# Pooled attention and a top-1 mixture of experts: the blocked token tiles of a slot scaled two slots ahead, their turns, casts and low parts in a chunk each, and flags read a slot earlier

## The chip, the cores and the metric

The kernel runs on one core of a Trainium2 chip. The time is device microseconds of one launch, with all inputs and the output in device memory. Timed runs are compared by their median; one further execution was profiled.

## The reference

Eight batches of eight heads attend over keys and values that were averaged in groups of eight. The result, 4608 tokens of 512, goes through a mixture of 8 experts, of which each token uses one.

```python
scores = scale * np.matmul(q, k_p.transpose(0, 1, 3, 2))      # k_p, v_p: means of 8 rows
attn = np.exp(scores - np.max(scores, axis=-1, keepdims=True))
attn = attn / (np.sum(attn, axis=-1, keepdims=True) + 1e-09)
x = np.matmul(attn, v_p)                                      # as [4608, 512]
...
logits = x @ w_gate + modality_bias[modality_id]
e_idx = np.argmax(logits, axis=1)
...
for e in range(E):
    mask = e_idx == e
    h = np.maximum(x[mask] @ w1[e], 0.0)
    out[mask] = gate_w[mask, None] * (h @ w2[e])
```

All is in 32 bit floats. w1[e] is 512 x 1024 and w2[e] 1024 x 512.

## The kernel before

The kernel has two stages. The first computes attention and the gates and writes each token's row to `xs` in DRAM: 512 values, its gate weight (column D) and eight factors, one a head (from column RX), by which its values are still to be multiplied. The second stage, the experts, is where the change lies.

**Slots and chunks.** Tokens are sorted by expert into slots of 256 (two tiles of 128 rows, `tt` 0 and 1). Slots 0 to 16 always run; slot 17 runs in one of several forms, here the one called `wide`, in which 384 tokens (a third tile, `xe`) are computed at once. A slot has 8 chunks, `f` 0 to 7, each of 128 hidden units. For a chunk, TensorE (PE) computes the hidden units (`hidden`, L193 and L196), and then the second layer of the chunk before (`second`, L1304), so that ScalarE (ACT) and VectorE (DVE) have one second layer's time to make the hidden units ready. Precision comes from splitting: a value is kept as a rounded high part and the low rest. So each chunk has a fixed chain: ACT copies a half of the sum (`ht`, L198), DVE adds the other half (L199), ACT takes the positive part and rounds it (`hh`, L200), DVE computes the low rest (`hlo`, L202).

**What else a slot needs.** Its tokens are gathered from `xs` by POOL (L144) into `xg`, a ring of four tiles, two a slot. From slot 5 on (`FIRST_BLOCKED`) a slot is "blocked": its tokens are turned (transposed) by DVE rather than by PE. `blocks_out` (L1219) multiplies each tile by its factors on DVE (four instructions, L1227, into a tile `xp` of its own), stores it through SP's queue to `scr` in DRAM (L1231), keeps the gate column in `gc` (L1214), and loads it again so that blocks of 32 x 32 lie where they belong (`y`, L1237). `blocks_turn` turns each block on DVE (L1243) and casts it on ACT (L1245, the high part in `xhl`, for slot 17 `xw`); `blocks_low` computes the low part on DVE (L1250).

**What sets the order.** The order on each engine is the order in which the program is written; each engine works its own list through, and waits by semaphores. `run` (L1342) writes one slot, chunk by chunk. In chunk 0 stand, for slot s + 1: `blocks_out`, the evacuation of the slot before (`tail`: `ob`, L1275 on DVE, L1277 on ACT, scattered by POOL, L1281), and `slot_flag`. The flag says whether slot s + 1 has another expert than slot s. ACT and DVE read it into a register (L1258), and at each chunk they branch on it (`changed`, L1309): if it is set, ACT splits the new weights' high part (L138) and DVE their low part (L141). The functions for the low part wait in a list, `lag`, and are taken up about two chunks later. In chunk 4 stand the gathers of slot s + 2 and the turn and cast of tile 0 of slot s + 1, in chunk 5 the low part of tile 0 and then the turn and cast of tile 1, and so on. Weights are loaded by SP's queue two slots ahead (L128, L131), under a condition, into `raw`.

The end of slot 16 and the first hidden layer of slot 17, which reads `xw`, are written by `close` and `wide`.

Of the kernel before, what the change touches and what calls it, by code (L numbers as in the profile page):

```python
# [9 lines left out]
F32 = mybir.dt.float32  # L10
# [5 lines left out]
ALU = mybir.AluOpType  # L16
# [6 lines left out]
P = 128  # L23
SLOT = 256
EARLY_GROUPS = 2
EARLY_SLOTS = 2
EXTRA = (128,)
QUAD = 32
FIRST_BLOCKED = 5
# [4 lines left out]
def kernel(  # L34
# [12 lines left out]
    nc = tc.nc  # L47
    ctx.enter_context(tc.manual_schedule(engines=ENGINES))
    B, H, S, HD = q.shape
    NTOK, D = out.shape  # L50
    E, _, FF = w1.shape
# [7 lines left out]
    ND = D // P  # L59
    XW = D + 16  # L60
    RX = D + 8
    NSTAT = NTOK // SLOT
# [28 lines left out]
    xg = [cp.tile([P, XW], F32, name=f"xg{i}") for i in range(4)]  # L91
# [57 lines left out]
    def gather(s, idx, col, xgs, rows=NTOK):  # L149
        for tt in range(2):  # L150
            gather_tile(xgs[(2 * s + tt) % 4], idx, col + tt, rows)
# [6 lines left out]
    def scale(s, xgs):  # L158
        for tt in range(2):
            scale_tile(xgs[(2 * s + tt) % 4])  # L160
# [3 lines left out]
    def tokens_of(s):  # L164
        return xhl[s % len(xhl)] if s != NSTAT - 1 else xw
# [52 lines left out]
    with ExitStack() as actx:  # L218
# [661 lines left out]
        for g in range(len(GROUPS) - 1):  # L880
            n = s1_of[2 * g + 1] + 2
# [74 lines left out]
        for n in range(N + 1):  # L956
            has, nxt, nxt2 = n < N, n + 1 < N, n + 2 < N
# [82 lines left out]
    mp = ctx.enter_context(tc.tile_pool(name="mp", bufs=1))  # L1040
# [3 lines left out]
    op = [[ps_op.tile([P, 512], F32, name=f"op{i}_{z}") for z in range(2)] for i in range(2)]  # L1044
# [9 lines left out]
    xe = xg[4]  # L1054
# [142 lines left out]
    def do_late(s, f):  # L1197
        for fn in late.get((s, f), ()):
            fn()

    scr = dram.tile([2, 3 * P, D], F32, name="scr")
    gc = mp.tile([P, NCOL], F32, name="gc")
    ys, yts = {}, {}
    NQ = P // QUAD

    def tts_of(s):
        return (0, 1) if s != NSTAT - 1 else (0, 1, 2)

    def blocked(s):
        return FIRST_BLOCKED <= s < NSTAT  # L1210

    def keep_gates(s, eng):
        for tt in range(2):
            eng.tensor_copy(gc[:, 2 * s + tt:2 * s + tt + 1], xg[(2 * s + tt) % 4][:, D:D + 1])  # L1214

    def gate_of(s, tt):
        return gc[:, 2 * s + tt:2 * s + tt + 1] if s > EARLY_SLOTS else xg[(2 * s + tt) % 4][:, D:D + 1]

    def blocks_out(s):  # L1219

        tts = tts_of(s)
        for tt in tts:
            x = xg[(2 * s + tt) % 4] if tt < 2 else xe
            xp = mp.tile([P, NQ, ND, QUAD], F32, tag="xp", bufs=2, name=f"xp_{s}_{tt}")
            f = x[:, RX:RX + H].rearrange("p (k a o q) -> p k a o q", a=2, o=1, q=1)
            for a in range(2):
                nc.vector.tensor_tensor(  # L1227
                    xp[:, 2 * a:2 * a + 2].rearrange("p j k r -> p k j r"),
                    x[:, 0:D].rearrange("p (k a j r) -> p a k j r", k=ND, a=2, j=2)[:, a],
                    f[:, :, a].to_broadcast([P, ND, 2, QUAD]), op=ALU.mult)  # L1230
            nc.sync.dma_start(scr[s % 2, tt * P:(tt + 1) * P, :], xp.rearrange("p j k r -> p (j k r)"))  # L1231
        keep_gates(s, nc.vector)
        n = len(tts) * NQ
        ys[s] = mp.tile([P, n, P], F32, tag="bid", name=f"y_{s}")
        src = scr[s % 2, 0:len(tts) * P, :].rearrange("(u c) (j x) -> j c u x", c=QUAD, j=NQ)
        for j in range(NQ):
            nc.sync.dma_start(ys[s][j * QUAD:(j + 1) * QUAD], src[j])  # L1237

    def blocks_turn(s, tt):
        ab = tokens_of(s)  # L1240
        sl = slice(tt * P, (tt + 1) * P)
        yt = yts[s, tt] = mp.tile([P, ND, P], F32, tag="bsel", name=f"yt_{s}_{tt}")
        nc.vector.transpose(yt.rearrange("p k (u c) -> p u k c", c=QUAD),  # L1243
                            ys[s][:, NQ * tt:NQ * (tt + 1), :].rearrange("p u (k r) -> p u k r", r=QUAD))
        nc.scalar.copy(ab[:, :, 0, sl], yt)  # L1245

    def blocks_low(s, tt):
        ab = tokens_of(s)
        sl = slice(tt * P, (tt + 1) * P)
        nc.vector.tensor_sub(ab[:, :, 1, sl], yts[s, tt], ab[:, :, 0, sl].bitcast(F32))  # L1250

    def slot_regs(s):
        load_regs(s, meta[0:1, 1 + s:2 + s], meta[0:1, 2 + NSLOT + s:3 + NSLOT + s])
# [3 lines left out]
    def slot_flag(s):  # L1257
        flags[s] = nc.values_load(meta[0:1, 2 + NSLOT + s:3 + NSLOT + s],  # L1258
                                  engines=[mybir.EngineType.Activation, mybir.EngineType.DVE], min_val=0, max_val=1,
                                  skip_runtime_bounds_check_because="a comparison's result")  # L1260

    def part(s):

        ab = tokens_of(s)
        o = op[s % 2]
        third = op[(s + 1) % 2][0]
        nxt, nxt2 = s + 1 < NSLOT, s + 2 < NSLOT
        early = s + 1 < EARLY_SLOTS
# [20 lines left out]
        def hidden(f, at=None, width=SLOT, **kw):  # L1289
            hh, hlo = at or (hhs[f % 2], hlos[f % 2])  # L1290
            if width > SLOT:
                first(f, ab, hp[f % 2][:, 0:width], hh[:, 0:width], hlo[:, 0:width])()
            else:
                first_wide(f, ab, hp[f % 2], hts[f % 2], hh[:, 0:SLOT], hlo[:, 0:SLOT], **kw)

        def second(f, tts=(0, 1), at=None, width=SLOT):
            hh, hlo = at or (hhs[f % 2], hlos[f % 2])
            if s == 0:
                hh, hlo = h0[f][:, 0, 0:SLOT], h0[f][:, 1, 0:SLOT]
            for tt in tts:  # L1300
                ts_ = slice(tt * P, min((tt + 1) * P, width))
                ot = o[tt] if tt < 2 else third[0:width - SLOT]
                for n, (l, w) in enumerate(((hh, 0), (hh, 1), (hlo, 0))):
                    nc.tensor.matmul(ot, l[:, ts_], hl[f][:, w, D:2 * D],  # L1304
                                     start=(f == 0 and n == 0), stop=(f == NF - 1 and n == 2))
# [36 lines left out]
        def run(fs, tail):  # L1342
            later = []
            for f in fs:
                def pop():
                    if len(lag) > 1 or (f == 1 and lag):
                        lag.pop(0)()
                if f:
                    hidden(f, between=pop)
                if f == 0:  # L1350
                    if blocked(s + 1):
                        blocks_out(s + 1)
                    if 0 < s < NSTAT - 1:
                        tail(later=later)
                    else:
                        tail()
                    if nxt and EARLY_SLOTS <= s < NSTAT - 1 and not blocked(s + 1):
                        gather(s + 1, gidx, 2 * (s + 1), xg)
                if f == 0:
                    pop()  # L1360
                do_late(s, f)
                if f == (0 if s >= EARLY_SLOTS else 1) and nxt and not early:
                    slot_flag(s + 1)
                if f == 0 and nxt2:
                    slot_regs(s + 2)
                if s == 1 and f == 2:
                    gather(s + 1, gidx, 2 * (s + 1), xg)

                if s >= NSTAT - 1 and f == CUT and nxt:
                    gather(s + 1, gidx, 2 * (s + 1), xg)  # L1370
                if f:
                    second(f - 1)
                    renew(f - 1)
                if f == (2 if blocked(s + 1) else 3 if EARLY_SLOTS <= s < NSTAT - 1 else 4) and nxt and not early:
                    if not blocked(s + 1):
                        scale(s + 1, xg)
                        if s + 1 > EARLY_SLOTS:
                            keep_gates(s + 1, nc.gpsimd)
                    while later:
                        later.pop(0)()  # L1380
                if f == 4 and blocked(s + 2):
                    gather(s + 2, gidx, 2 * (s + 2), xg)
                    if s + 2 == NSTAT - 1:
                        gather_tile(xe, gidx, 2 * NSTAT)
                if s == NSTAT - 2 and f == 4:
                    nc.gpsimd.drain()
                if blocked(s + 1):
                    for tt in tts_of(s + 1):
                        if f == 4 + tt:
                            blocks_turn(s + 1, tt)  # L1390
                        if f == 5 + tt:
                            blocks_low(s + 1, tt)
                elif f == (5 if EARLY_SLOTS <= s < NSTAT - 1 else 6) and nxt:
                    x_transposes(s + 1, xg)
                if f == NF - 1 and s != NSTAT - 2:
                    close()
# [65 lines left out]
    sl = mp.tile([P, 1], I32, name="sl")  # L1462
# [84 lines left out]
```

## Time and profile before

| what | value |
|---|---|
| timed runs, median of 3 | 622.5 us (622.03 to 623.03) |
| the profiled execution | 624.98 us, span 623.3 us |
| granted TensorE clock, mean | 0.994 |
| TensorE matmul busy | 587.8 us, 94% of the span |
| VectorE, ScalarE, GpSimd busy | 366.1, 271.4, 194.3 us |
| expert stage | from about 185 us to the end |

Lines of the timeline read: start in us, duration in us, engine, line, operation, output <- input, partitions x elements, how many instructions were merged, and in brackets the idle time of the engine before it with what ended it. "ACTq L1309" and "DVEq L1309" are instructions of the sequencers of ACT and DVE that are filed under the branch at L1309: where PE waits for "ACTq L1309", it waits for ACT's part of the chain above. A line of the table of stretches reads: from:to and length, then the busy time of PE, PE's weight loads, DVE, ACT and POOL with the number of instructions, the granted clock, the share of the DMA engines and GB/s. A page shows matmuls as longer than their distance, since they are pipelined; so the times of chunks are taken from start to start.

### The profile page before, as it was taken

The page shows a single profiled execution, that of the slowest core. Times are in us where ns is not written, and L with a number is a line of the kernel's source. Part 1 is how long each engine was busy: PE and PEld are TensorE (multiplying, and loading weights), DVE is VectorE, ACT ScalarE, POOL GpSimd, SP SyncE. Part 2 cuts the span into 40 slices and gives each one's busy share as a digit, 9 for nine tenths or more (in the row PEclk, how much of TensorE's full clock was granted, in tenths as well). Part 3 has the DMA queues.
Part 4 walks back from the last instruction along what each step waited for, and adds up shares of the span by engine and source line. Part 5 has one row for each costly group of instructions (what it writes and reads, how often), then busy time and mean ns, then how long its engine had stood idle before and what let it go on. Part 6 is the DMA issues. An engine that isn't in the chain of part 4 may idle for free. (4 is left out here: it accounts for less than half of the span.)

```text
span 623.3 us, 12231 instructions
## 1 busy us (share of the span) xinstructions
PE 587.8 (94%) x3555; PEld 502.3 (81%) x3555; DVE 366.1 (59%) x922; ACT 271.4 (44%) x653; POOL 194.3 (31%) x302
## 2 busy tenths in 40 slices
PE   5899999999999999999999999999999989989895
PEld 4789889888898888887878877778878868877794
DVE  6757798789958455464454457654454585454311
ACT  2666576788541233333333246333333553333210
POOL 6689968663000340511211211301201211300101
PEclk9999899999999999999999999999999999999899
DMA  8999969884212720331431764422426812414001
GB/s 253 301 295 319 358 182 370 260 267 136 58 45 83 250 74 31 104 90 49 137 87 52 201 191 152 135 72 67 136 75 204 247 66 78 142 64 85 35 2 54
DMA packets 79650, 90.50 MB, mean 145 GB/s; under 512 B 16655, under 2 KB 55055, under 8 KB 79568
## 3 DMA queue, kind: packets, MB, share of 16 engines
q1 hardware_dynamic: 73648, 70.14, 36.8%
q0 software_dynamic: 5920, 19.44, 10.1%
q8 instruction: 30, 0.49, 0.3%
q14 instruction: 52, 0.43, 0.2%
HBM read 122.02 MB, written 26.53 MB: 238 GB/s over the span
## 5 line engine op out<-in xcount | busy, mean ns | idle before, releaser
L1304 PE MATMUL op<-hl,hh 128*128 128x512 f32 x512 | 164.2, 402 | 10.8 <-ACTq L1309 8.7
L193 PE MATMUL hp<-xhl,hl 128*128 128x512 f32 x512 | 137.8, 391 | 0.0
L1281 POOL DMA_INDIRECT out_dram<-ob,sidx x36 | 38.4, 1068 | 293.3 <-DVEq L1309 168.7
L199 DVE TENSOR_TENSOR ht<-ht,hp 128x256 f32<-128x256 f32 x128 | 53.8, 420 | 113.8 <-ACT ht L198 88.7
L193 PEld LDWEIGHTS hp<-xhl,hl 128*128 128x128 f32 x512 | 95.8, 188 | 20.8
L1304 PEld LDWEIGHTS op<-hl,hh 128*128 128x128 f32 x512 | 88.0, 190 | 25.8 <-ACTq L1309 12.6
L1304 PE MATMUL op<-hl,hlo 128*128 128x512 f32 x256 | 100.9, 394 | 1.2 <-DVE hlo L202 1.2
L200 ACT ACTIVATE hh<-ht 128x256 fp32r<-128x256 f32 x128 | 53.5, 418 | 94.1 <-DVE ht L199 68.6
L198 ACT COPY ht<-hp 128x256 f32<-128x256 f32 x128 | 47.4, 370 | 98.3 <-PE hp L196 78.5
L202 DVE SCALAR_TENSOR_TENSOR hlo<-ht,hh 128x256 fp32r<-128x256 f32 x128 | 54.9, 429 | 55.7 <-ACTq L1309 48.4
L196 PEld LDWEIGHTS hp<-xhl,hl 128*128 128x128 f32 x512 | 78.2, 189 | 10.2
L196 PE MATMUL hp<-xhl,hl 128*128 128x256 f32 x512 | 81.2, 281 | 0.0
L1304 PEld LDWEIGHTS op<-hl,hlo 128*128 128x128 f32 x256 | 48.2, 188 | 17.7 <-DVE hlo L202 7.6
L144 POOL DMA_INDIRECT xg<-xs,gidx x36 | 37.9, 1054 | 49.0 <-DVEq L1309 17.5
L645 PE MATMUL av<-vw,pt 128*128 128x146 f32 (+1 forms) x320 | 50.7, 298 | 1.9 <-ACT pt L615 1.1
L645 PEld LDWEIGHTS av<-vw,pt 128*128 128x128 f32 (+1 forms) x320 | 40.7, 183 | 4.1 <-ACT pt L615 2.2
L581 PE MATMUL sc<-kt,qt 128*128 128x144 f32 x256 | 37.3, 289 | 1.0 <-ACT qt L562 1.0
L581 PEld LDWEIGHTS sc<-kt,qt 128*128 128x128 f32 x256 | 33.1, 190 | 1.7 <-ACT qt L562 0.9
L588 DVE TENSOR_REDUCE mx<-sc 128x8 f32<-128x576 f32 (+1 forms) x40 | 27.7, 692 | 8.9 <-PE sc L581 6.8
L649 PE MATMUL av<-vw,pt 128*128 128x146 f32 (+1 forms) x160 | 31.2, 295 | 0.3
L1245 ACT CAST xhl<-yt 128x512 fp32r<-128x512 f32 x24 | 14.9, 621 | 34.8 <-DVE yt L1243 34.8
L591 DVE TENSOR_TENSOR sb<-sc,mx 128x576 f32<-128x576 f32 (+1 forms) x40 | 27.7, 693 | 2.5 <-DVE mx L588 0.6
(267 smaller groups left out, 835.7 us busy)
## 6 DMA issues: line engine op xcount, KB each, us to landing
raw<-in_moe_w_dram SPq DMA_DIRECT2D x288, 256.0 KB
xs<-xb SPq DMA_DIRECT2D x16, 528.0 KB
k<-in_k_dram SPq DMA_DIRECT2D x7, 1024.0 KB
v<-in_v_dram SPq DMA_DIRECT2D x7, 1024.0 KB
q<-in_q_dram SPq DMA_DIRECT2D x7, 1024.0 KB
scr<-xp SPq DMA_DIRECT2D x27, 256.0 KB
y<-scr SPq DMA_DIRECT2D x48, 128.0 KB
v<-in_v_dram SPq DMA_DIRECT2D x16, 128.0 KB
```

The lines of the kernel that those rows point to most:

```text
L144: nc.gpsimd.indirect_dma_start(out=x, out_offset=None, in_=xs[0:rows, :], in_offset=IndirectOffsetOnAxis(idx[:, col:col + 1].bitcast(U32), 0),
L193: nc.tensor.matmul(ph, hl[f][:, 0, d * P:(d + 1) * P], ab[:, d, :, 0:SLOT], start=(d == 0), stop=False)
L196: nc.tensor.matmul(ph[:, 0:SLOT], hl[f][:, 1, d * P:(d + 1) * P], ab[:, d, 0, 0:SLOT], start=False, stop=(d == ND - 1))
L198: nc.scalar.copy(t, ph[:, SLOT:2 * SLOT])
L199: nc.vector.tensor_add(t, t, ph[:, 0:SLOT])
L200: nc.scalar.activation(hh, t, AF.Relu)
L202: nc.vector.scalar_tensor_tensor(hlo, t, 0.0, hh.bitcast(F32), op0=ALU.max, op1=ALU.subtract)
L581: nc.tensor.matmul(dst, qt[:, i, :], kt[b % NB][:, :, h * SPL:(h + 1) * SPL], start=True, stop=True)
L645: nc.tensor.matmul(av[hs, u, 2 * VC * gg:2 * VC * (gg + 1)], pt[:, c, hs], vw[y][:, c].rearrange("p a x -> p (a x)"), start=(gg == 0), sto ...
L649: nc.tensor.matmul(dst4[hs], pt4[:, hs], v4[y][:, 2 * u:2 * u + 2, :], start=False, stop=True)
L1281: nc.gpsimd.indirect_dma_start(out=out[:, :], out_offset=IndirectOffsetOnAxis(idx.bitcast(U32), 0), in_=ob, in_offset=None, bounds_check=N ...
L1304: nc.tensor.matmul(ot, l[:, ts_], hl[f][:, w, D:2 * D], start=(f == 0 and n == 0), stop=(f == NF - 1 and n == 2))
```

## The change

The diff, cut to its core:

```diff
-    def blocks_out(s):
-        tts = tts_of(s)
-        for tt in tts:
-            x = xg[(2 * s + tt) % 4] if tt < 2 else xe
-            xp = mp.tile([P, NQ, ND, QUAD], F32, tag="xp", bufs=2, name=f"xp_{s}_{tt}")
...
-            nc.sync.dma_start(scr[s % 2, tt * P:(tt + 1) * P, :], xp.rearrange("p j k r -> p (j k r)"))
-        keep_gates(s, nc.vector)
-        n = len(tts) * NQ
-        ys[s] = mp.tile([P, n, P], F32, tag="bid", name=f"y_{s}")
+    def blocks_out(s, tt):
+        x = xg[(2 * s + tt) % 4] if tt < 2 else xe
+        xp = xg[(2 * s + 2 + tt % 2) % 4][:, 0:D].rearrange("p (j k r) -> p j k r", j=NQ, r=QUAD)
...
+        if tt < 2:
+            keep_gate(s, tt, nc.vector)
+        rows = scr[s % 2, tt * P:(tt + 1) * P, :]
+        nc.sync.dma_start(rows, xg[(2 * s + 2 + tt % 2) % 4][:, 0:D])
+        if tt == 0:
+            ys[s] = mp.tile([P, len(tts_of(s)), NQ, P], F32, tag="bid", name=f"y_{s}")
...
         for j in range(NQ):
-            nc.sync.dma_start(ys[s][j * QUAD:(j + 1) * QUAD], src[j])
+            nc.sync.dma_start(ys[s][j * QUAD:(j + 1) * QUAD, tt], src[j])
...
-        yt = yts[s, tt] = mp.tile([P, ND, P], F32, tag="bsel", name=f"yt_{s}_{tt}")
+        yt = yts[s, tt] = mp.tile([P, ND, P], F32, tag=("bsel", "yt")[tt % 2], name=f"yt_{s}_{tt}")
...
-        nc.scalar.copy(ab[:, :, 0, sl], yt)
+    def blocks_high(s, tt):
+        nc.scalar.copy(tokens_of(s)[:, :, 0, tt * P:(tt + 1) * P], yts[s, tt])
...
                 if f == 0:
-                    if blocked(s + 1):
-                        blocks_out(s + 1)
...
-                if f == (0 if s >= EARLY_SLOTS else 1) and nxt and not early:
+                if f == 1 and s == EARLY_SLOTS - 1:
                     slot_flag(s + 1)
+                if f == 1 and s >= EARLY_SLOTS - 1 and nxt2:
+                    slot_flag(s + 2)
...
-                if f == 4 and blocked(s + 2):
+                if f == (2 if s + 2 > FIRST_BLOCKED else 4) and blocked(s + 2):
                     gather(s + 2, gidx, 2 * (s + 2), xg)
...
                         if f == 4 + tt:
+                            blocks_low(s + 1, tt)
+                        if f == 3 + tt:
+                            blocks_high(s + 1, tt)
+                        if f == 2 + tt:
                             blocks_turn(s + 1, tt)
-                        if f == 5 + tt:
-                            blocks_low(s + 1, tt)
-                elif f == (5 if EARLY_SLOTS <= s < NSTAT - 1 else 6) and nxt:
+                if blocked(s + 2) and f in (6, 7):
+                    blocks_out(s + 2, f - 6)
+                if blocked(s + 1) and f == 0 and len(tts_of(s + 1)) > 2:
+                    blocks_out(s + 1, 2)
```

Scaling goes from chunk 0 of the slot before (both tiles at once) to chunks 6 and 7 of two slots before, a tile each; only slot 17's third tile stays in chunk 0 of slot 16. The scaled values no longer go to a tile `xp`, but into the ring tiles of the slot between, whose own tokens have been used by then; the gathers that fill those next stand in chunk 2. Turn, cast and low part of tile 0 stand in chunks 2, 3 and 4, of tile 1 in 3, 4 and 5. The flag of slot s + 2 is read in chunk 1 of slot s. The loads of `y` are half as large and twice as many.

DVE at the boundary into slot 7, before the change: the scaling for slot 8, two gates, the evacuation of slot 6, one low part of weights (run only if the flag is set), the flag's read (TENSOR_LOAD), and the add of chunk 1.

```order
L1227 TENSOR_TENSOR xp_0_4573<-xg_80 128x4x2x32 x2
L1227 TENSOR_TENSOR xp_1_4577<-xg_81 128x4x2x32 x2
L1214 COPY gc<-xg_80 128x1
L1214 COPY gc<-xg_81 128x1
L1275 TENSOR_SCALAR ob_0_4588<-op_0_2815,gc 128x512
L1309 COMPARE_AND_BRANCH
L1309 UNCONDITIONAL_BRANCH
L141 TENSOR_TENSOR hl_2255<-raw_3022,hl_2255 128x1024
L1309 UNCONDITIONAL_BRANCH
L1258 TENSOR_LOAD meta
L199 TENSOR_TENSOR ht_2822<-ht_2822,hp_2820 128x256
```

The same place after the change, from the low rest of chunk 0 to the add of chunk 1:

```order
L202 SCALAR_TENSOR_TENSOR hlo_2825<-ht_2821,hh_2823 128x256
L1308 COMPARE_AND_BRANCH
L1308 UNCONDITIONAL_BRANCH x2
L1274 TENSOR_SCALAR ob_0_4600<-op_0_2815,gc 128x512
L1308 COMPARE_AND_BRANCH
L1308 UNCONDITIONAL_BRANCH
L141 TENSOR_TENSOR hl_2255<-raw_3022,hl_2255 128x1024
L1308 UNCONDITIONAL_BRANCH
L199 TENSOR_TENSOR ht_2822<-ht_2822,hp_2820 128x256
```

Only the evacuation and the low part of weights are left there; scaling, gates and the flag's read have gone.

DVE in chunks 4 to 6 of slot 7 before the change, from the turn of slot 8's tile 0 to the add of chunk 6:

```order
L1243 STREAM_TRANSPOSE yt_0_4714<-y_4583 128x4x4x32
L199 TENSOR_TENSOR ht_2822<-ht_2822,hp_2820 128x256
L1309 COMPARE_AND_BRANCH
L1309 UNCONDITIONAL_BRANCH
L141 TENSOR_TENSOR hl_1998<-raw_3013,hl_1998 128x1024
L1309 UNCONDITIONAL_BRANCH
L202 SCALAR_TENSOR_TENSOR hlo_2826<-ht_2822,hh_2824 128x256
L1309 COMPARE_AND_BRANCH
L1309 UNCONDITIONAL_BRANCH x2
L1250 TENSOR_TENSOR xhl_86<-yt_0_4714,xhl_86 128x4x128
L1243 STREAM_TRANSPOSE yt_1_4742<-y_4583 128x4x4x32
L199 TENSOR_TENSOR ht_2821<-ht_2821,hp_2819 128x256
```

After the change, in chunks 2 to 4 of the same slot, from the turn of tile 0 to the add of chunk 4:

```order
L1240 STREAM_TRANSPOSE yt_0_4678<-y_4543 128x4x4x32
L199 TENSOR_TENSOR ht_2822<-ht_2822,hp_2820 128x256
L1308 COMPARE_AND_BRANCH
L1308 UNCONDITIONAL_BRANCH
L141 TENSOR_TENSOR hl_1772<-raw_3007,hl_1772 128x1024
L1308 UNCONDITIONAL_BRANCH
L202 SCALAR_TENSOR_TENSOR hlo_2826<-ht_2822,hh_2824 128x256
L1308 COMPARE_AND_BRANCH
L1308 UNCONDITIONAL_BRANCH x2
L1240 STREAM_TRANSPOSE yt_1_4705<-y_4543 128x4x4x32
L199 TENSOR_TENSOR ht_2821<-ht_2821,hp_2819 128x256
```

Between two adds there is now one instruction of the tiles, where there were two in chunk 5.

SP's queue before the change, behind chunk 0, where slot 8's tiles are stored and loaded again:

```order
L1231 DMA scr<-xp_0_4573 128x512
L1231 DMA scr<-xp_1_4577 128x512
L1309 UNCONDITIONAL_BRANCH x3
L1237 DMA y_4583<-scr 32x8x128
L1309 UNCONDITIONAL_BRANCH
L1237 DMA y_4583<-scr 32x8x128
L1309 UNCONDITIONAL_BRANCH
L1237 DMA y_4583<-scr 32x8x128
L1309 UNCONDITIONAL_BRANCH
L1237 DMA y_4583<-scr 32x8x128
```

After the change, in chunks 6 and 7 of slot 6, from the load of tile 0 (its store stands just ahead of it) to the store of tile 1; the rows of L128 and L131 are weight loads:

```order
L1236 DMA y_4543<-scr 32x4x128
L1308 UNCONDITIONAL_BRANCH
L1236 DMA y_4543<-scr 32x4x128
L1308 UNCONDITIONAL_BRANCH
L1236 DMA y_4543<-scr 32x4x128 x2
L128 ISA
L128 DMA raw_3019<-in_moe_w_dram 128x4x128
L1308 UNCONDITIONAL_BRANCH x2
L131 ISA
L131 DMA raw_3019<-in_moe_w_dram 128x512
L1231 DMA scr<-xg_83 128x512
```

The two stores stood together with four loads of 128 KB behind them; now the second store stands behind the first tile's loads and a pair of weight loads.

More of the change, by code (lines that the diff above doesn't have):

```diff
@@ L1210, in blocked, with keep_gate @@
         return FIRST_BLOCKED <= s < NSTAT
-    def keep_gates(s, eng):
-        for tt in range(2):
-            eng.tensor_copy(gc[:, 2 * s + tt:2 * s + tt + 1], xg[(2 * s + tt) % 4][:, D:D + 1])
+    def keep_gate(s, tt, eng):
+        eng.tensor_copy(gc[:, 2 * s + tt:2 * s + tt + 1], xg[(2 * s + tt) % 4][:, D:D + 1])
     def gate_of(s, tt):
         return gc[:, 2 * s + tt:2 * s + tt + 1] if s > EARLY_SLOTS else xg[(2 * s + tt) % 4][:, D:D + 1]
-    def blocks_out(s):
-        tts = tts_of(s)
-        for tt in tts:
-            x = xg[(2 * s + tt) % 4] if tt < 2 else xe
-            xp = mp.tile([P, NQ, ND, QUAD], F32, tag="xp", bufs=2, name=f"xp_{s}_{tt}")
[L1225 to L1231, printed above, removed]
-        keep_gates(s, nc.vector)
-        n = len(tts) * NQ
-        ys[s] = mp.tile([P, n, P], F32, tag="bid", name=f"y_{s}")
-        src = scr[s % 2, 0:len(tts) * P, :].rearrange("(u c) (j x) -> j c u x", c=QUAD, j=NQ)
@@ new lines, in blocks_out @@
+    def blocks_out(s, tt):
+        x = xg[(2 * s + tt) % 4] if tt < 2 else xe
+        xp = xg[(2 * s + 2 + tt % 2) % 4][:, 0:D].rearrange("p (j k r) -> p j k r", j=NQ, r=QUAD)
+        f = x[:, RX:RX + H].rearrange("p (k a o q) -> p k a o q", a=2, o=1, q=1)
+        for a in range(2):
+            nc.vector.tensor_tensor(
+                xp[:, 2 * a:2 * a + 2].rearrange("p j k r -> p k j r"),
+                x[:, 0:D].rearrange("p (k a j r) -> p a k j r", k=ND, a=2, j=2)[:, a],
+                f[:, :, a].to_broadcast([P, ND, 2, QUAD]), op=ALU.mult)
+        if tt < 2:
[4 more added lines that the diff above has]
+            ys[s] = mp.tile([P, len(tts_of(s)), NQ, P], F32, tag="bid", name=f"y_{s}")
+        src = rows.rearrange("(u c) (j x) -> j c u x", c=QUAD, j=NQ)
@@ L1236, in blocks_out @@
         for j in range(NQ):
-            nc.sync.dma_start(ys[s][j * QUAD:(j + 1) * QUAD], src[j])
+            nc.sync.dma_start(ys[s][j * QUAD:(j + 1) * QUAD, tt], src[j])
     def blocks_turn(s, tt):
-        ab = tokens_of(s)
-        sl = slice(tt * P, (tt + 1) * P)
-        yt = yts[s, tt] = mp.tile([P, ND, P], F32, tag="bsel", name=f"yt_{s}_{tt}")
+        yt = yts[s, tt] = mp.tile([P, ND, P], F32, tag=("bsel", "yt")[tt % 2], name=f"yt_{s}_{tt}")
         nc.vector.transpose(yt.rearrange("p k (u c) -> p u k c", c=QUAD),
-                            ys[s][:, NQ * tt:NQ * (tt + 1), :].rearrange("p u (k r) -> p u k r", r=QUAD))
@@ L1245, in blocks_turn @@
-        nc.scalar.copy(ab[:, :, 0, sl], yt)
+                            ys[s][:, tt].rearrange("p u (k r) -> p u k r", r=QUAD))
+    def blocks_high(s, tt):
+        nc.scalar.copy(tokens_of(s)[:, :, 0, tt * P:(tt + 1) * P], yts[s, tt])
     def blocks_low(s, tt):
@@ L1377, in run @@
                         if s + 1 > EARLY_SLOTS:
-                            keep_gates(s + 1, nc.gpsimd)
+                            for tt in range(2):
+                                keep_gate(s + 1, tt, nc.gpsimd)
                     while later:
                         later.pop(0)()
-                if f == 4 and blocked(s + 2):
+                if f == (2 if s + 2 > FIRST_BLOCKED else 4) and blocked(s + 2):
                     gather(s + 2, gidx, 2 * (s + 2), xg)
@@ L1389, in run @@
                         if f == 4 + tt:
+                            blocks_low(s + 1, tt)
+                        if f == 3 + tt:
+                            blocks_high(s + 1, tt)
+                        if f == 2 + tt:
                             blocks_turn(s + 1, tt)
-                        if f == 5 + tt:
-                            blocks_low(s + 1, tt)
-                elif f == (5 if EARLY_SLOTS <= s < NSTAT - 1 else 6) and nxt:
+                if blocked(s + 2) and f in (6, 7):
+                    blocks_out(s + 2, f - 6)
+                if blocked(s + 1) and f == 0 and len(tts_of(s + 1)) > 2:
+                    blocks_out(s + 1, 2)
+                if not blocked(s + 1) and f == (5 if EARLY_SLOTS <= s < NSTAT - 1 else 6) and nxt:
                     x_transposes(s + 1, xg)
```

## Prediction

> **What bounds the kernel now.** First the page's busy shares, then a table of stretches over the expert stage, then the timeline inside single chunks.
>
> ```profile
> PE 587.8 (94%) x3555; PEld 502.3 (81%) x3555; DVE 366.1 (59%) x922; ACT 271.4 (44%) x653; POOL 194.3 (31%) x302
> 274.56:577.47 302.91, 290.98 (x1429) 239.19 (x1427) 164.59 (x372) 117.71 (x257) 54.34 (x51) 1.00 0.40 119
> 563.39:574.47 11.08, 11.08 (x58) 9.42 (x56) 4.99 (x10) 3.45 (x9) 1.00 (x1) 1.00 0.45 87
> ```
>
> TensorE bounds the kernel. The last row holds four chunks of slot 16 in which PE is never idle: 11.08 / 4 = 2.77 us a chunk, at a granted clock of 1.00. The row above runs from chunk 2 of slot 4 to the end of chunk 7 of slot 16, 12 slots of 8 chunks and 6 more, 102 in all. At 2.77 they would take 282.5 us; they take 302.9. So **20.4 us** of this stretch are stalls (with the slower start after each), and only PE's stalls count. This is what one undisturbed chunk looks like:
>
> ```profile
> 566.17 1.07 PE L193 MATMUL hp<-xhl,hl 128*128 128x512 f32 x4
> 567.80 0.37 ACT L198 COPY ht<-hp 128x256 f32<-128x256 f32 x1 [1.49 <-PE hp L196]
> 568.21 0.42 DVE L199 TENSOR_TENSOR ht<-ht,hp 128x256 f32<-128x256 f32 x1 [1.44 <-ACT ht L198]
> 568.66 0.42 ACT L200 ACTIVATE hh<-ht 128x256 fp32r<-128x256 f32 x1 [0.49 <-DVE ht L199]
> 569.11 0.42 DVE L202 SCALAR_TENSOR_TENSOR hlo<-ht,hh 128x256 fp32r<-128x256 f32 x1 [0.48 <-ACT hh L200]
> 570.31 0.40 PE L1304 MATMUL op<-hl,hh 128*128 128x512 f32 x1
> ```
>
> Counted from the chunk's first matmul, ACT copies at 1.63, DVE adds at 2.04 and is free at 3.36, hh is ready at 2.91, and PE wants it at 4.14. DVE's next add is due at 2.77 + 2.04 = 4.81, so 1.45 us lie free on DVE in each chunk, and hh has 1.23 us to spare: about 2.6 us of other DVE work fit between two chunks before PE stands. The trace holds a test of this, early in slot 2, where the routing table puts one long instruction there:
>
> ```profile
> 226.69 1.07 PE L193 MATMUL hp<-xhl,hl 128*128 128x512 f32 x4
> 227.22 1.80 DVE L1111 TENSOR_TENSOR bsel<-iota_f,col 128x1584 bf16<-128x1584 f32 x1
> 229.46 0.84 PE L193 MATMUL hp<-xhl,hl 128*128 128x512 f32 x3
> ```
>
> 1.80 us more on DVE, and PE's chunk is still 2.77 us. That boundary too has an evacuation and a flag read, but no blocks to scale.
>
> **The change part by part.** *The slot boundary* (here into slot 5):
>
> ```profile
> 295.99 1.43 DVE L1227 TENSOR_TENSOR xp<-xg 128x256 f32<-128x256 f32 x4
> 297.34 0.21 DVE L1214 COPY gc<-xg 128x1 f32<-128x1 f32 x2
> 297.47 0.74 DVE L1275 TENSOR_SCALAR ob<-op,gc 128x512 f32<-128x512 f32 x1
> 299.20 0.42 DVE L199 TENSOR_TENSOR ht<-ht,hp 128x256 f32<-128x256 f32 x1 [1.00 <-DVEq L1309]
> 300.12 0.73 PE L1304 MATMUL op<-hl,hh 128*128 128x512 f32 x2 [0.38 <-ACTq L1309]
> ```
>
> Scaling and gates take 297.47 - 295.99 = 1.48 us, the evacuation 0.74, the flag read 0.99 (298.21 to 299.20): 3.2 us where 2.6 fit, so PE stalls some 0.6 us, in 13 slots. The change leaves the evacuation alone there. Each tile's scaling with its gate, 1.48 / 2 = 0.74 us, goes to a chunk of its own (6 and 7), and the flag read, 0.99 us on DVE and as much at most on ACT, goes behind chunk 1. Each is below the 1.80 us that cost PE nothing. If that cover is gone, the price is their own length less 2.6, still nothing. Slot 1 reads two flags: between nothing and 2 x 0.99 = 2.0 us of DVE, one time, under 2.6; I take nothing.
>
> *Chunks 4 to 6* (slot 4):
>
> ```profile
> 285.65 0.62 ACT L1245 CAST xhl<-yt 128x512 fp32r<-128x512 f32 x1 [1.25 <-DVE yt L1243]
> 286.27 1.07 PE L193 MATMUL hp<-xhl,hl 128*128 128x512 f32 x4
> 288.54 0.71 DVE L1243 STREAM_TRANSPOSE yt<-y 128x512 f32<-128x512 f32 x1
> 289.29 0.62 ACT L1245 CAST xhl<-yt 128x512 fp32r<-128x512 f32 x1 [1.84 <-DVE yt L1243]
> 289.81 0.37 ACT L198 COPY ht<-hp 128x256 f32<-128x256 f32 x1
> 291.14 0.73 PE L1304 MATMUL op<-hl,hh 128*128 128x512 f32 x2 [0.55 <-ACTq L1309]
> ```
>
> ACT stands before each cast until DVE has turned the tile, and its copy of the next chunk waits behind: at 289.81, where an undisturbed one is due 1.63 after that chunk's start, at 287.90. The delay outgrows hh's spare, and PE stalls. With turn, cast and low part in three successive chunks the cast finds its tile ready and takes 0.62 us in ACT's gap (2.91 + 0.17 to 4.40, over 1.3 us). DVE gets 0.71 or less a chunk. So this stall goes too.
>
> *Into slot 16* a third tile is scaled, and its buffer has to come free first:
>
> ```profile
> 556.36 3.32 SPq L1231 DMA_DIRECT2D scr<-xp  x3
> 558.57 0.76 DVE L1227 TENSOR_TENSOR xp<-xe 128x256 f32<-128x256 f32 x2 [1.56 <-DMA scr<-xp]
> 561.90 0.73 PE L1304 MATMUL op<-hl,hh 128*128 128x512 f32 x2 [2.57 <-ACTq L1309]
> ```
>
> The store lands 558.57 - 556.36 = 2.2 us after its issue; DVE waits, PE loses 2.6 us. Afterwards only that third scaling (0.76) is left beside the evacuation, into a buffer whose store is five chunks old: 1.5 us, nothing lost.
>
> *The start of slot 17* waits for the third tile's cast and low part, which will be done a chunk or two earlier:
>
> ```profile
> 578.71 0.93 PE L183 MATMUL hp<-xw,hl 128*128 128x384 f32 x4 [1.24 <-ACT xw L1245]
> 580.86 2.65 PE L183 MATMUL hp<-xw,hl 128*128 128x384 f32 x8 [1.22 <-DVE sl L1437]
> 577.47:585.30 7.83, 5.38 (x19) 4.68 (x19) 3.00 (x7) 1.80 (x4) 0.00 (x0) 0.78 0.01 2
> 585.30:588.80 3.50, 3.50 (x20) 3.23 (x19) 0.82 (x2) 1.18 (x2) 0.98 (x1) 1.00 0.20 75
> 577.80:581.20 3.40, 1.27 (x6) 0.99 (x7) 1.62 (x5) 1.31 (x3) 0.00 (x0) 1.00 0.02 5
> 557.30:560.70 3.40, 2.03 (x11) 1.55 (x9) 1.54 (x5) 0.00 (x0) 0.31 (x1) 1.00 0.56 207
> ```
>
> The first wide layer and one second layer took 7.83 us; the next pair, as many matmuls, 3.50. So **4.3 us** are lost: 2.46 idle, and 1.87 to a granted clock of 0.78, right after 3.4 us in which PE worked 1.27. The Trainium skill, "TensorE: Matmul & The Clock Gate", section "What's actually happening", lets activity over free-running windows of about 3.4 us halve or release the clock. By that rule the dip goes with the idle time; if it came anyway, the sum would be 1.9 us smaller. The trace agrees in part: 2.03 busy us in 3.4 (last row) brought no dip. I take the dip as gone.
>
> *What may stay.* In slots 8, 9, 13 and 14 new weights are split as well:
>
> ```profile
> 380.04:396.80 16.76, 15.21 (x71) 11.64 (x70) 14.49 (x27) 9.49 (x18) 1.75 (x1) 1.00 0.27 93
> 498.41:515.13 16.72, 15.15 (x71) 11.65 (x70) 14.55 (x27) 9.46 (x17) 1.75 (x1) 1.00 0.24 83
> 392.70 1.22 DVE L141 TENSOR_TENSOR hl<-raw,hl 128x1024 fp32r<-128x1024 f32 x1
> 393.83 0.42 DVE L199 TENSOR_TENSOR ht<-ht,hp 128x256 f32<-128x256 f32 x1
> ```
>
> Five chunks take 16.76 and 16.72 instead of 13.85: 5.8 of the 20.4 us. A split adds 1.13 us between L200 and L202, of which 0.48 hide in DVE's wait for ACT: DVE is then free from 4.0 to 4.81, 0.8 us a chunk, and the new pieces take 0.7. It fits barely, and in chunks 0 to 2, with evacuation or flag and split together, it runs up to half a microsecond late, which hh's spare covers. I leave 0.6 us for each of the two, between 0 (all fits) and 2.9 (nothing gained).
>
> *DMA and queues.* Stores stay 27; the loads of y go from 52 to 108 of half the size, all on SP, whose other work is weight loads two slots ahead. The gathers now overwrite buffers whose stores must have landed:
>
> ```profile
> 249.52 1.05 POOL L144 DMA_INDIRECT xg<-xs,gidx  x1 [12.85 <-DVEq L1309]
> 253.22 1.04 POOL L155 TENSOR_TENSOR xg<-xg 128x512 f32<-128x512 f32 x1 [1.11 <-DMA xg<-xs,gidx]
> 298.48 1.03 POOL L1281 DMA_INDIRECT out_dram<-ob,sidx  x1 [16.03 <-DVEq L1309]
> 302.71 1.00 POOL L1281 DMA_INDIRECT out_dram<-ob,sidx  x1 [3.20 <-DMA out_dram<-ob,sidx]
> ```
>
> A gather lands 253.22 - 249.52 = 3.7 us after its issue; the two scatters stand 4.2 us apart. With the evacuation done 1.3 us into chunk 1, the gathers issue some 7.1 and 8.5 us and land 10.8 and 12.2 us into it; the scalings that want them come at 17.2 and 20.0. The second store, issued near the start of the next chunk 1, lands 3 us into it, before the 7.1. POOL and DVE have room.
>
> Sum: 20.4 + 4.3 - 1.2 = **23.5 us**. The profiled execution took 625.0 us (span 623.3), 2.5 above the median of the timed runs; the gain is a difference in one execution, so I take it from the median: 622.5 - 23.5 = **599.0**.
>
> **The rivals.**
> *Weight slots and the dip stay.* Their chunks have little room: 20.4 + 4.3 - 5.8 - 1.9 = 17.0, so 605.5.
> *The flag read is the stall.* If ACT and DVE stood for it wherever it is put, 13 slots keep 0.99: 23.5 - 12.9 = 10.6, so 611.9. Against it speaks slot 2, where a flag read and an evacuation cost PE nothing.
> *Slower: the loads of y come late.* SP stores tile 0, waits for its landing (2.2), issues four loads, two weight loads, and only then the second store; tile 1's loads go out 3 to 5 us into chunk 1, and its turn stands on DVE at 8.9. If they landed within 2.2, 1.5 us would be left, and 1.9 more that the chunk can bear. From 5.6 us of landing PE stalls; from 5.6 + 23.5 / 13 = 7.4 us on the kernel is slower than before, at 9 us by 13 x 1.6 = 21, so 643. No row shows when y lands; a store, the nearest, took 2.2. The Trainium skill, "DMA: Bandwidth & Descriptors", section "Rules for kernel authors", advises to join small transfers and calls those under 64 KB mostly overhead, and these shrink from 128 KB to about that; no run here shows it.
> *No gain:* PE's stalls come from something the change doesn't move, 622.5. The rows above name their causes too plainly for much of this.
>
> **How the numbers follow.** Forecast 0.70 (597 to 602), weight slots and dip 0.17, flag 0.05, no gain 0.04, slower 0.04. The range goes from all 24.7 us gone and the runs' spread (597.0) to the second case with half a microsecond (606.0), and leaves out 0.13. A difference under 0.2% can't be told from none here: faster 0.92, same 0.04, slower 0.04.
>
> **What would show it.** Right: chunks of 2.77 across boundaries and in chunk 7, PE nearly without idle time from slot 4 to 17, no wait of the casts for yt, no clock below 1.00 near the start of slot 17. Wrong: DVE waiting at the scaling for a gather or at a turn for y, PE still waiting for hh in chunk 1 or 2 of plain slots, or stalls that move into the chunks with L141.

## The result, and the profile after

| | before | changed |
|---|---|---|
| median of the timed runs | 622.76 us (622.03 to 623.36) | 601.37 us (599.15 to 603.24) |
| ratio | | 0.9656, 95% interval 0.9618 to 0.9693 |
| the profiled execution, and its span | 624.98, 623.3 us | 599.15, 597.1 us |

The kernel is 21.4 us faster by the medians (622.76 - 601.37). A second set of runs of the changed kernel gave 601.36 us, ratio 0.9645 (0.9617 to 0.9673). The changed kernel's profiled execution was the fastest of its runs, the one of before lay 2.2 us above its median, so the two spans differ by more: 26.2 us.

The profile of the changed kernel: busy shares, the group of second-layer matmuls (its last field is PE's idle time ahead of them; the same group of before stands below it), and five stretches.

```profile
PE 577.5 (97%) x3555; PEld 500.7 (84%) x3555; DVE 366.1 (61%) x922; ACT 273.8 (46%) x653; POOL 196.6 (33%) x302
...
L1303 PE MATMUL op<-hl,hh 128*128 128x512 f32 x512 | 161.4, 397 | 1.1 <-ACT hh L200 1.1
```

```profile
L1304 PE MATMUL op<-hl,hh 128*128 128x512 f32 x512 | 164.2, 402 | 10.8 <-ACTq L1309 8.7
```

```profile
270.95:556.09 285.14, 283.50 (x1430) 239.93 (x1428) 166.10 (x370) 121.00 (x260) 54.18 (x50) 1.00 0.40 125
556.09:559.58 3.49, 3.49 (x19) 3.23 (x18) 1.18 (x4) 0.64 (x2) 0.00 (x0) 1.00 0.00 0
0.00:50.00 50.00, 42.29 (x350) 37.51 (x350) 34.08 (x71) 29.38 (x79) 39.85 (x101) 1.00 1.01 293
195.91:270.95 75.04, 74.99 (x448) 63.66 (x446) 40.68 (x105) 25.88 (x61) 24.25 (x25) 1.00 0.35 116
559.58:597.10 37.52, 31.67 (x157) 27.85 (x155) 6.02 (x10) 4.82 (x9) 4.90 (x5) 0.96 0.10 37
```

And three stretches of before that answer to the last three:

```profile
0.00:50.00 50.00, 39.33 (x327) 34.32 (x328) 33.24 (x65) 27.46 (x74) 37.34 (x97) 1.00 0.97 279
199.51:274.56 75.05, 75.00 (x448) 63.66 (x447) 39.51 (x101) 25.50 (x60) 21.73 (x24) 1.00 0.33 109
585.30:623.30 38.00, 31.69 (x157) 27.87 (x155) 5.67 (x10) 4.82 (x9) 4.90 (x5) 0.99 0.10 37
```

The same 102 chunks now take 285.14 instead of 302.91 us, 17.8 less, with 2.6 us left above 102 x 2.77. The start of slot 17 takes 3.49 instead of 7.83 us, 4.3 less, all of it at full clock. The end is 0.5 us shorter. The remaining 3.6 us (chunk 2 of slot 4 starts at 270.95 instead of 274.56) come from ahead of that point: from chunk 1 of slot 1 to chunk 2 of slot 4 both kernels take 75.0 us, and already in the first 50 us PE was 3 us busier in this execution. They are a difference between two executions, not between two kernels: the second profile of the same changed kernel reaches chunk 2 of slot 4 at 274.01. So 22.6 us of the 26.2 belong to the change.

A plain slot of the changed kernel, DVE and ACT in chunks 2 and 3 of slot 6 (timeline):

```profile
318.63 0.71 DVE L1240 STREAM_TRANSPOSE yt<-y 128x512 f32<-128x512 f32 x1
320.02 0.42 DVE L199 TENSOR_TENSOR ht<-ht,hp 128x256 f32<-128x256 f32 x1 [0.68 <-ACT ht L198]
...
321.15 0.62 ACT L1244 CAST xhl<-yt 128x512 fp32r<-128x512 f32 x1 [0.26 <-issue]
322.39 0.37 ACT L198 COPY ht<-hp 128x256 f32<-128x256 f32 x1 [0.61 <-PE hp L196]
```

The turn lies in DVE's gap, and the add after it still waits 0.68 us for ACT, not ACT for it. The cast no longer waits for a turn, and ACT then waits 0.61 us for PE. That is how a chunk looks in which PE is never kept waiting.

What is left lies in slot 8 (and, smaller, in slot 13): SP, DVE and PE.

```profile
358.99 0.37 SPq L131 DMA_DIRECT2D raw<-in_moe_w_dram  x1
359.57 0.25 SPq L1231 DMA_DIRECT2D scr<-xg  x1
363.28 1.99 SPq L1236 DMA_DIRECT2D y<-scr  x4
...
368.87 0.71 DVE L1240 STREAM_TRANSPOSE yt<-y 128x512 f32<-128x512 f32 x1 [2.69 <-DMA y<-scr]
...
370.39 0.73 PE L1303 MATMUL op<-hl,hh 128*128 128x512 f32 x2 [1.07 <-ACT hh L200]
```

Tile 1's store was issued at 359.57, behind weight loads that run in this slot. The loads of y start when it has landed, 3.7 us later (in a plain slot 2.05, 312.95 to 315.00), and they land 3.6 us after the last of them was issued (363.28 + 1.99 to 368.87). DVE stands 2.69 us at the turn, the add of the next chunk waits behind it, and PE waits for hh; the chunk takes 4.66 us instead of 2.77.

### The profile page after: what moved, and what is told of

The parts are those of the page before. It is cut to its first block, busy times and chain, and to the rows that moved or that the text cites. A ratio compares the mean times of both kernels' runs of the same rounds, so it can differ in the third digit from the quotient of the medians.

```text
span 597.1 us, 12324 instructions
## 1 busy us (share of the span) xinstructions
PE 577.5 (97%) x3555; PEld 500.7 (84%) x3555; DVE 366.1 (61%) x922; ACT 273.8 (46%) x653; POOL 196.6 (33%) x302
## 5 line engine op out<-in xcount | busy, mean ns | idle before, releaser
L1303 PE MATMUL op<-hl,hh 128*128 128x512 f32 x512 | 161.4, 397 | 1.1 <-ACT hh L200 1.1
L193 PEld LDWEIGHTS hp<-xhl,hl 128*128 128x128 f32 x512 | 95.8, 188 | 20.4
L645 PE MATMUL av<-vw,pt 128*128 128x146 f32 (+1 forms) x320 | 49.4, 293 | 2.3 <-DVE xb L678 1.2
L649 PE MATMUL av<-vw,pt 128*128 128x146 f32 (+1 forms) x160 | 30.1, 291 | 0.3
L141 DVE TENSOR_TENSOR hl<-raw,hl 128x1024 fp32r<-128x1024 f32 x24 | 29.0, 1217 | 0.0
```

The costliest lines, as they stand in the source:

```text
L193: nc.tensor.matmul(ph, hl[f][:, 0, d * P:(d + 1) * P], ab[:, d, :, 0:SLOT], start=(d == 0), stop=False)
L645: nc.tensor.matmul(av[hs, u, 2 * VC * gg:2 * VC * (gg + 1)], pt[:, c, hs], vw[y][:, c].rearrange("p a x -> p (a x)"), start=(gg == 0), sto ...
L649: nc.tensor.matmul(dst4[hs], pt4[:, hs], v4[y][:, 2 * u:2 * u + 2, :], start=False, stop=True)
L1303: nc.tensor.matmul(ot, l[:, ts_], hl[f][:, w, D:2 * D], start=(f == 0 and n == 0), stop=(f == NF - 1 and n == 2))
```

## The experiments

Theory: DVE has some 2.6 us of room between two chunks; a boundary stalled because scaling (1.48), evacuation (0.74) and flag read (0.99) together outgrew it, and chunks 6 and 7 stalled because ACT stood before a cast whose tile was not yet turned. Rivals: one of the parts is a stall by itself, wherever it stands, and the rest did nothing. Each time below is the median of timed runs; the kernel before, run beside them, took 622.54 us in the first four and 623.15 in the last three.

### Flags read in chunk 0 again

```diff
-                if f == 1 and s == EARLY_SLOTS - 1:
-                    slot_flag(s + 1)
-                if f == 1 and s >= EARLY_SLOTS - 1 and nxt2:
-                    slot_flag(s + 2)
+                if f == (0 if s >= EARLY_SLOTS else 1) and nxt and not early:
+                    slot_flag(s + 1)
```

> The changed kernel, but flags are read in chunk 0 for the next slot, as before. Theory (DVE has 2.6 us of room between two chunks; evacuation 0.74 and flag read 0.99 make 1.7): as fast as the change, about 601 us, and PE idle at no plain boundary. Rival (the flag read where it stood was the stall): 13 boundaries lose 0.5 to 1.0 us again, 608 to 614 us.

Measured: 599.77 us, ratio 0.9662 (0.9619 to 0.9704), the same as the change. DVE at the boundary of a plain slot:

```profile
292.15 0.75 DVE L1274 TENSOR_SCALAR ob<-op,gc 128x512 f32<-128x512 f32 x1
293.89 0.42 DVE L199 TENSOR_TENSOR ht<-ht,hp 128x256 f32<-128x256 f32 x1 [0.99 <-ACT ht L198]
```

The flag read is back between these two rows, the add comes 0.99 us after the evacuation, and PE waits for nothing from there on. The flag by itself is no stall, and once scaling has left the boundary, moving the flag brings nothing that can be measured.

### Flags alone

The edit is the one above, turned round, in the kernel before.

> The kernel before with nothing changed but the flags (read in chunk 1 for two slots on). Theory of room: plain boundaries fall from 3.2 us of DVE work to 2.2 and stall no more; of the 11.3 us at boundaries 1.2 each at slots 9 and 14 and about 1.9 at slot 16 stay: about 7 us faster, 615.5 us. Rival (scaling is the stall by itself, the flag read costs nothing): 622 us.

Measured: 612.83 us, ratio 0.9853 (0.982 to 0.9885), 9.7 us faster, 2.7 more than expected. DVE at the same boundary, where scaling still stands:

```profile
294.62 1.43 DVE L1227 TENSOR_TENSOR xp<-xg 128x256 f32<-128x256 f32 x4
295.97 0.21 DVE L1214 COPY gc<-xg 128x1 f32<-128x1 f32 x2
296.09 0.74 DVE L1275 TENSOR_SCALAR ob<-op,gc 128x512 f32<-128x512 f32 x1
297.17 0.42 DVE L199 TENSOR_TENSOR ht<-ht,hp 128x256 f32<-128x256 f32 x1 [0.33 <-DVEq L1309]
```

The add comes 0.34 us after the evacuation instead of 0.99, and PE is idle at no plain boundary; its idle time stays at slots 9, 14 and 16, at the casts, and at the start of slot 17. (The chunks at the boundaries in slots 4 and 8 still take 0.3 us longer, without a wait that shows.) So neither flag nor scaling is a stall: at a plain boundary either one alone fits, and taking away either one is enough. Nor was all of the 0.99 us the flag's read: 0.34 of it stay without it.

In the profile the surplus lies at the casts, which this edit doesn't touch. From start to start, the 13 chunks at the boundaries lost 11.3 us before and lose 5.4 here; chunks 5 to 7 lost 8.6 before and lose 6.0 here, though ACT still waits 34.5 us for turns. The start of chunk 4 of slot 7 and ACT's copy in it, before and then here:

```profile
350.66 1.07 PE L193 MATMUL hp<-xhl,hl 128*128 128x512 f32 x4
353.03 0.37 ACT L198 COPY ht<-hp 128x256 f32<-128x256 f32 x1 [2.23 <-PE hp L196]
```

```profile
346.89 1.07 PE L193 MATMUL hp<-xhl,hl 128*128 128x512 f32 x4
348.52 0.38 ACT L198 COPY ht<-hp 128x256 f32<-128x256 f32 x1 [1.48 <-PE hp L196]
```

Before, the copy came 2.37 us after the chunk's start, 0.74 later than in an undisturbed chunk, ahead of both casts; chunk 7 then took 3.58 us. Here it comes at 1.63, and chunk 7 takes 2.86. So in a plain slot the wait for the turns alone costs 0.1 us, and more only where ACT is late already: before in most plain slots, by up to 0.8 us, here in slot 4 alone. Why ACT is late there, no row shows.

This execution also had no clock dip at slot 17, although PE stood there as before. That doesn't explain the median: the other three runs had a mean granted clock of 0.993 to 0.996, against 0.999 here, and took 612.0 to 613.5 us, against 612.65.

### Scaling at the boundary again

The kernel before with the new flags (the part of the edit shown above) and with turns, casts and low parts a chunk each; cut to the order in the slot:

```diff
...
-                        if f == 4 + tt:
-                            blocks_turn(s + 1, tt)
                         if f == 5 + tt:
                             blocks_low(s + 1, tt)
+                        if f == 4 + tt:
+                            blocks_high(s + 1, tt)
+                        if f == 3 + tt:
+                            blocks_turn(s + 1, tt)
```

> Scaling in chunk 0 of the slot before, both tiles at once into tiles of their own, as before the change; flags as in the change; turns, casts and low parts a chunk each, from chunk 3. Theory of room: scaling and evacuation alone are 2.2 us, which fit into 2.6, so plain boundaries are free; what stays is 1.2 us each at slots 9 and 14 and about 1.9 at slot 16, and the 2.7 us of late y go: about 603 us. Rival (scaling at the boundary is the stall by itself): the 11.3 us of all boundaries come back, about 610 us.

Measured: 604.5 us, ratio 0.9729 (0.9694 to 0.9764). PE's waits from slot 1 to the start of slot 17 (us in total, times, longest):

```profile
PE op L1306 <- issue: 2.0, 1, 2.0
PE op L1306 <- ACT hh L200: 0.8, 2, 0.4
PE op L1306 <- DVE hlo L202: 0.6, 2, 0.3
PE hp L183 <- DVE xw L1252: 0.4, 1, 0.4
```

One wait of 2.0 at slot 16, two of 0.4 with 0.3 behind each at slots 9 and 14, 0.4 at slot 17, and none elsewhere: the list that was expected, but for the 0.4. So what moving the scaling adds to the other two parts is those few places, 3.1 us of medians (604.5 - 601.4), and not the ten plain boundaries.

### Turn and cast in one chunk again

```diff
                         if f == 4 + tt:
-                            blocks_low(s + 1, tt)
-                        if f == 3 + tt:
-                            blocks_high(s + 1, tt)
-                        if f == 2 + tt:
                             blocks_turn(s + 1, tt)
+                            blocks_high(s + 1, tt)
+                        if f == 5 + tt:
+                            blocks_low(s + 1, tt)
```

> The changed kernel, but turn and cast of a tile stand in the same chunk (4 and 5, slot 17's third tile 6), the low part a chunk later, as before. Theory (ACT standing before a cast until the tile is turned is a stall of its own): the 8.7 us in chunks 6 and 7 and the 4.3 us at slot 17's start come back, the 2.7 us in which the turn waited for y in slots 8 and 13 go: about 611 to 612 us. Rival (only the work at the boundary counted, ACT's wait is hidden): 601 to 603 us.

Measured: 609.72 us, ratio 0.9811 (0.9777 to 0.9845), 8.4 us slower than the change, 2 short of what was expected. ACT's wait for the turn is back, and so is PE's in chunk 6 of several slots and at the start of slot 17 (one group of ACT's waits, and PE's waits):

```profile
ACT xhl L1244 <- DVE yt L1240: 33.2, 24, 1.7
```

```profile
PE op L1303 <- ACTq L1308: 1.3, 4, 0.5
PE hp L183 <- DVE sl L1442: 1.2, 1, 1.2
PE op L1303 <- ACT hh L200: 0.9, 2, 0.5
PE hp L183 <- ACT xw L1244: 0.8, 1, 0.8
PE op L1303 <- DVE hlo L202: 0.6, 2, 0.3
```

The start of slot 17 has its 2.0 us of idle time again, but the clock did not fall in this execution: 1.9 of the 4.3 us expected there did not come. Of the time that the 102 chunks lose, some 5 us lie in slots 8, 9, 13 and 14, where weights are split, and some 2.4 in plain slots.

### The change again, and scaling a chunk earlier

```diff
-                if blocked(s + 2) and f in (6, 7):
-                    blocks_out(s + 2, f - 6)
+                f0 = 6 if s + 2 == FIRST_BLOCKED else 5
+                if blocked(s + 2) and f in (f0, f0 + 1):
+                    blocks_out(s + 2, f - f0)
```

> The changed kernel once more, to stand beside the next two. About 601 us, runs from 598 to 604. Theory (the turn of tile 1 waits for y where weights are loaded): the turns' wait for y is found in slots 8 and 13 alone, between nothing and 2.7 us each, and differs from run to run. Rival (it was a chance of one profiled execution): no turn waits for y.

> The changed kernel with scaling, store and loads of y one chunk (2.77 us) earlier, in chunks 5 and 6 instead of 6 and 7 (slot 5 as before). Theory of late y: the largest wait, 2.7 us, is just covered; no turn waits, PE has no stall in slots 8 and 13, 1 to 3 us faster than the change beside it. Rival (splitting weights on DVE and ACT is what stalls slots 8 and 13): low part of tile 1 and a scaling now stand in one chunk, so those slots get worse by about 1 us; no gain or a small loss.

Measured: the change 601.36 us (599.15 to 602.09), ratio 0.9645 (0.9617 to 0.9673); with scaling earlier 598.43 us (596.21 to 600.41), ratio 0.9607 (0.9578 to 0.9636). DVE's waits for y in the change, then in the earlier version:

```profile
DVE yt L1240 <- DMA y<-scr: 3.4, 1, 3.4
DVE yt L1240 <- DMA raw<-in_moe_w_dram: 0.4, 1, 0.4
```

```profile
DVE yt L1240 <- DMA y<-scr: 0.3, 1, 0.3
```

This time the change waited 3.4 us in slot 8 and not in slot 13 (in the first profile 2.7 and 1.6), so the late turn differs from run to run, as the theory had it. A chunk earlier it is gone, PE waits nowhere in the stretch, and the kernel is 2.9 us faster by the medians; the two intervals overlap a little, but the direction is that of the trace. Low part and scaling now share a chunk in the weight slots, and that cost nothing that shows: splitting was not what stalled them. By its median this version is the fastest here.

### Scaling a chunk later

```diff
-                if blocked(s + 2) and f in (6, 7):
-                    blocks_out(s + 2, f - 6)
+                if blocked(s + 2) and f == 7:
+                    blocks_out(s + 2, 0)
+                if blocked(s + 1) and f == 0:
+                    blocks_out(s + 1, 1)
```

> The changed kernel with scaling, store and loads of y one chunk later, tile 0 in chunk 7 and tile 1 in chunk 0 of the next slot, beside the evacuation (1.5 us, which fits). Theory of late y: in slots 8 and 13 the turn of tile 1 is 2.8 us later than in the change, so each loses about 2.8 us more, about 605 to 608 us; in plain slots y comes about 1.3 us late, which the chunk can bear, so little or nothing. Rival (stalls of slots 8 and 13 are splitting): no more than the change, 600 to 603 us.

Measured: 623.75 us, ratio 1.0018 (0.9996 to 1.0041): all that the change brings is gone. SP, DVE and PE in a plain slot, and DVE's wait in total:

```profile
299.52 0.36 SPq L1231 DMA_DIRECT2D scr<-xg  x1
301.56 3.24 SPq L1236 DMA_DIRECT2D y<-scr  x4
308.17 0.71 DVE L1240 STREAM_TRANSPOSE yt<-y 128x512 f32<-128x512 f32 x1 [4.16 <-DMA y<-scr]
309.69 0.73 PE L1303 MATMUL op<-hl,hh 128*128 128x512 f32 x2 [1.98 <-ACTq L1308]
```

```profile
DVE yt L1240 <- DMA y<-scr: 41.1, 13, 6.7
```

The mechanism was the expected one, the size was not: 13 turns wait, 3.2 us each on average, in plain slots too, and PE loses some 26 us in the 102 chunks. My expectation took a landing of 2.2 us for y, as of a store; here y lands 3.4 us after the last load was issued (301.56 + 3.24 to 308.17), 6.6 after the first.

## Why the prediction was right, point by point

- **PE bounds, and its stalls are the gain.** Right. Of the 20.4 us in the 102 chunks 17.8 went, and undisturbed chunks stayed at 2.77 us.
- **The boundary: 3.2 us of work into 2.6 of room.** Shown from both sides: with the flag alone taken away, and with the scaling alone put back, plain boundaries are free. The prediction named both as moved and did not say that either would do. It took all of the 0.99 us for the flag; without the read 0.34 of them stay.
- **The casts.** Shown by putting them back: 33.2 us of ACT's waits and 8.4 us of time. That the wait for the turn alone outgrows hh's spare did not hold in plain slots: alone it delays ACT's copy by 1.17 us (2.80 instead of 1.63 after the chunk's start, flags alone) and costs 0.1 us. In slot 4, from which the prediction took its 1.91 us of delay, ACT was 0.75 late before the casts. The stall is the sum of the two; the cause of the second stays open.
- **Slot 17's start: 4.3 us.** In the profiled execution it went from 7.83 to 3.49 us, to a hundredth as worked out. Whether the medians hold all of it is not shown: 1.9 of it are a clock dip, which two other kernels did not have in their profiles with the same idle place. Of the timed runs only the mean granted clock is known: in the second set 0.989 to 0.996 for the kernel before (17 runs, mean 0.993) and 0.995 to 0.999 for the change (5 runs, mean 0.997). From these means, as an estimate, the kernel before loses 4.5 us of its span to the clock and the change 1.9, so on average a dip or more did go, at slot 17 or elsewhere.
- **Slots 8 and 13: 1.2 us left over for splitting weights.** Right place, wrong cause and less than half the size. Splitting fits; the 2.6 us that stayed come from turns that wait for y, as the slower rival had it, though only where weight loads delay store and loads. The step that was off is the bound of 2.2 us on y's landing, taken from a store in a quiet slot: it was 3.6 us here, behind a store of 3.7.
- **The slower rival** came nearer than its chance said. It needed y to land 7.4 us after its issue to cost more than the change brings. Moved one chunk, 2.77 us, to the later side, the kernel is at 623.75: the change stood one chunk from that edge.

Sum: 23.5 predicted, 21.4 measured by the medians. The known share of the difference is 1.4 us of late y beyond the 1.2 left over; the other 0.7 us are less than these runs can tell apart (the change alone went from 599.2 to 603.2).

## What to carry to other kernels

Measure the room first: in a stall-free chunk, the gap of the helping engine plus the spare time of its result is what may be put there, and a single stall is best read as a sum that outgrew it; then look for any one part that can leave. On engines that work in order, a consumer in the same step as its producer on another engine makes the whole queue wait, and one step between them cost a buffer here and no time. Where a transfer's landing stands in no row, put the wait for it where a doubled landing time would still fit, since the edge may lie one step away.

## What the runs showed of the hardware that was not expected

**The clock dip does not follow from the idle time alone.** PE's granted clock in stretches of about 3.4 us and in the one after each: at slot 17's start with the casts put back, then with the flags alone changed; then at slot 16 with scaling at the boundary.

```profile
563.10:566.50 3.40, 1.42 (x8) 1.10 (x8) 1.51 (x4) 1.31 (x3) 0.00 (x0) 1.00 0.02 5
566.50:569.90 3.40, 3.40 (x19) 3.14 (x19) 1.22 (x2) 1.19 (x2) 0.07 (x1) 1.00 0.00 0
```

```profile
567.35:570.76 3.41, 1.15 (x5) 0.86 (x6) 1.76 (x5) 1.31 (x3) 0.00 (x0) 1.00 0.02 5
570.76:574.20 3.44, 3.44 (x19) 3.17 (x19) 1.22 (x2) 1.04 (x2) 0.00 (x0) 1.00 0.00 0
```

```profile
540.40:543.90 3.50, 1.47 (x9) 1.11 (x7) 1.97 (x7) 0.42 (x1) 0.96 (x1) 1.00 0.43 159
543.90:547.30 3.40, 3.39 (x8) 2.72 (x9) 1.26 (x3) 0.79 (x2) 0.35 (x2) 0.50 0.88 198
```

With 1.42 and 1.15 busy us in the worst 3.4 us no dip followed; with 1.47 one did, 3.4 us at a clock of 0.50, as after the 1.27 us of before. These stretches were laid where PE was least busy, not where the chip counts. The Trainium skill, "TensorE: Matmul & The Clock Gate", section "What's actually happening", says that the activity window runs freely; the rows fit that: about the same idle time cost 1.7 us or nothing. That it goes by where the idle time falls is a reading; no run here lays the same stall at another place of the window. The prediction's test of the rule, one stretch with a dip and one without, could not have told this.

**Ahead of the change, executions of one kernel differ by 3 us.** The two profiled executions of the changed kernel start chunk 2 of slot 4 at 270.95 and at 274.01 us, 3.1 apart; the kernel before, at 274.56, lies 3.6 from the first. The timed runs of the kernel before went from 619.5 to 624.8 us. A profile's span is then a poor measure of a change of a few microseconds; the stretch in which the change acts is a good one.
